# Turning q and k of two batches by 32x32 blocks on VectorE, with block copies in DRAM ahead of it

## The chip, the cores and the metric

The kernel runs on one core of a Trainium2 chip. The metric is the device time of one execution in microseconds (us); less is better. Where a profile is read, one execution was recorded by the hardware profiler, and its times count from the start of its span. TensorE does matrix products into PSUM, VectorE and ScalarE do elementwise work and read PSUM, GpSimd (POOL) does elementwise work on SBUF and issues indirect DMAs, and SyncE (SP) issues plain DMAs.

## The reference

Two parts, one after the other, in float32. First, linear attention with decay over q, k, v of shape (4 batches, 8 heads, 768 rows, 64):

```python
for b in range(nb):                      # blocks of 64 rows
    intra = np.einsum('bhic,bhjc->bhij', qb, kb) * Dmask
    intra = np.einsum('bhij,bhjd->bhid', intra, vb)
    inter = np.einsum('bhid,bhde->bhie', qb * lam_pow, kv_state)
    out[:, :, sl] = intra + inter
    kv_state = lam_block * kv_state + np.einsum('bhsd,bhse->bhde', kb_dec, vb)
```

The heads are then laid side by side: x has shape (4, 768, 512). Second, Fourier mixing and an MLP:

```python
mixed = np.real(np.fft.fft(np.fft.fft(x, axis=1), axis=2))
u = x + mixed
un = (u - mean(u)) / sqrt(var(u) + 1e-6)          # over the last axis
return u + np.maximum(un @ w_ch1, 0.0) @ w_ch2    # 512 -> 2048 -> 512
```

The weights come as float64; the kernel reads their bits and converts them on the chip.

## The kernel before, in words

**Attention.** `attn_chunk` (L257) handles 128 rows of one batch with all 8 heads; a batch has six chunks. It loads k, q and v of the chunk (L261, one DMA each, in runs of 256 B). The products of q and k need the head dimension on the partitions, so TensorE transposes k and q against an identity matrix, four 128x128 pieces each (L272, L277), and ScalarE copies the results to SBUF as kT and qT (L274, L279). VectorE makes qs, q with its decay, from the PSUM tile of q (L282). Then come the scores (L290), their decay on VectorE (sc, L294), the state update (L305, L309, L310), where kd, k with its decay, is made by GpSimd (L268), the two products into the output (L318 from qs and the state, L322 from sc and v), a copy oT (L325), and transposes back to row order (L329). ScalarE stores the result x to a scratch in DRAM, and indirect gathers on GpSimd fetch mirrored rows (`mirror_a` L377 and L380, `mirror_b` L385).

**Fourier part.** `fft_ln` folds rows with their mirror rows on VectorE (`fold_x`, L365 to L368, then L405 to L416), takes the transform over the rows as matrix products (L440), copies it out (L444), takes the transform over the width (`width`, L453 to L458, three row groups and one last row), adds it to x (L519 to L523), and normalises (`norm`: L470, L471, L474, L475, L487). For the first four pairs of batch and row group the result is transposed by TensorE (L492) for the MLP. For the other eight it is turned by blocks on VectorE (uq, L497) and written to DRAM (utd, L501), and the rows themselves go to DRAM as ud (L507).

**MLP, in two forms.** `mlp` (L549) does those first four pairs plainly: 64 products of the first weight (L555) with ReLU by ScalarE and VectorE in turn (L563, L561), and two lots of 16 products of the second (L569), each lot followed by the sum with x (L575, L576) and a store. Rows of the first half go out by a plain DMA on SP (L543), the mirrored rows by an indirect DMA on GpSimd (L545). `late` (L623) does the other eight pairs in four rounds with a scheme of seven products in place of eight on 2x2 blocks; it needs sums of the weights (`combine_weights`, L614) and of the inputs (us, L627 to L630), and its products are L637 and L684.

**What sets the order.** The program is written as generators that yield an estimated cost, and `weave` runs two of them side by side in a given ratio (L758 to L773). Weight conversion (L227 to L240) is woven into the first 190 us, the first form of the MLP into what is left of the attention and Fourier parts, `combine_weights` into the end of that MLP (L779). A scheduler in the build then orders the instructions of each engine by its own estimate of when their operands are there, and gives each engine a fixed list. Pools set how many tiles of a name exist: x has ten buffers in rotation (L127), y has one (L574), the loads of k, q and v have two.

Of the kernel before, what the change touches and what calls it, by code (L numbers as in the profile page):

```python
# [75 lines left out]
def kernel(  # L76
# [131 lines left out]
    w1v = moe_w_ch1.rearrange("(c p) f -> p c f", p=128)  # L208
    w2v = moe_w_ch2.rearrange("(c p) m -> p c m", p=128)
    WP = 512  # L210

    def load_tables(i):
        if i == 1:
# [5 lines left out]
    def load_weights(dst, src):  # L219

        if src.dtype == F32:
            nc.sync.dma_start(dst, src)
            return
        raw = hp_.tile([128, 2 * WP], U32, tag="hr", name=f"raw{cnt[0]}")
        pw = ep.tile([128, WP], U16, tag="pw", name=f"pw{cnt[0]}")
        cnt[0] += 1
        nc.sync.dma_start(raw, src.bitcast(U32))  # L227
        lo, hi = raw[:, 0:2 * WP:2], raw[:, 1:2 * WP:2]
        top = raw.bitcast(U16)[:, 3:4 * WP:4]
        lof, d = lo.bitcast(F32), dst.bitcast(U32)  # L230

        nc.vector.tensor_scalar(pw, top, 0x7FF0, None, op0=ALU.bitwise_and)
        nc.scalar.activation(pw, pw, AF.Relu, bias=cvt[:, 0:1], scale=-1.0)
        nc.scalar.activation(pw, pw, AF.Relu, bias=cvt[:, 1:2], scale=-8.0)
        nc.vector.scalar_tensor_tensor(pw, top, 0x8000, pw, op0=ALU.bitwise_and, op1=ALU.bitwise_or)  # L235

        nc.vector.tensor_scalar(d, hi, 0x000FFFFF, None, op0=ALU.bitwise_and)
        nc.scalar.activation(lof, lo, AF.Copy, scale=2.0 ** -52)
        nc.vector.scalar_tensor_tensor(dst, d, 2.0 ** -20, lof, op0=ALU.mult, op1=ALU.add)  # L239
        nc.vector.scalar_tensor_tensor(dst, dst, 1.0, pw.bitcast(BF16), op0=ALU.add, op1=ALU.mult)  # L240
# [8 lines left out]
            yield 1.0  # L249


    xs, xn_, xd = {}, {}, {}

    def pair(t, hp):
        return t[:, 2 * hp:2 * hp + 2, :].rearrange("p a d -> p (a d)")

    def attn_chunk(b, c):  # L257
        rows = slice(c * C, (c + 1) * C)
        kt, qt, vt = (new(ld, [C, H, D], nm) for nm in ("k", "q", "v"))
        for t, src in ((kt, k), (qt, q), (vt, v)):  # L260
            nc.sync.dma_start(t, src[b, :, rows, :].rearrange("h p d -> p h d"))  # L261
        if b == 0:
            load_tables(c)

        last = c == NC - 1
        if not last:
            kd = new(at, [C, H, D], "kd")
            nc.gpsimd.tensor_tensor(kd, kt, kpow, op=ALU.mult)  # L268

        ptk = psum_a([128, HP, C])  # L270
        for hp in range(HP):
            nc.tensor.transpose(ptk[:, hp, :], pair(kt, hp), ident)  # L272
        kT = new(at, [128, HP, C], "kT", bufs=2)
        nc.scalar.copy(kT, ptk)  # L274
        ptq = psum_a([128, HP, C])
        for hp in range(HP):
            nc.tensor.transpose(ptq[:, hp, :], pair(qt, hp), ident)  # L277
        qT = new(at, [128, HP, C], "qT", bufs=2)
        nc.scalar.copy(qT, ptq)  # L279
        if c > 0:  # L280
            qs = new(at, [128, HP, C], "qs")
            nc.vector.tensor_tensor(qs, ptq, qpow, op=ALU.mult)  # L282
        yield 1.2


        mm = nc.tensor.matmul
# [68 lines left out]
        nc.gpsimd.memset(t, 0.0)  # L355

    gather = nc.gpsimd.indirect_dma_start
    eo, r1s = {}, {}

    def fold_x(b, a, n, i, lo, hi):  # L360

# [8 lines left out]
    def mirror_a(b):  # L370

        xa = xd[b][0]
        r1 = r1s[b] = [new(fp, [128, DM], f"r{a}") for a in range(2)]

        eo[b] = [(new(fp, [128, 2, 2 * W], f"fe{a}"), new(fp, [128, 2, 2 * W], f"fo{a}")) for a in range(2)]
        for a, n in enumerate(BLK):
            gather(out=r1[a][0:n], out_offset=None, in_=xa[:, :], in_offset=row_of(a, n))  # L377
        for t in range(2, HC):
            u = xs[b, HC + t] = new(xp, [128, DM], "x")
            gather(out=u[:, :], out_offset=None, in_=xa[:, :], in_offset=row_of(2 + t))  # L380
# [6 lines left out]
            xs[b, t] = xn_.pop((b, t))  # L387

    def fold_a(b):
        r1 = r1s.pop(b)  # L390
        for a, n in enumerate(BLK):
            fold_x(b, a, n, 1, r1[a][0:n], xn_[b, HC + a][0:n])

    def fold_b(b):

# [145 lines left out]
    def store(b, T, y, cols=slice(0, DM)):  # L541
        if T < HC:
            nc.sync.dma_start(out[b, 128 * T:128 * T + 128, cols], y[:, cols])  # L543
        else:
            nc.gpsimd.indirect_dma_start(out=out.rearrange("b s d -> (b s) d"),  # L545
                                         out_offset=row_of(2 + HC * (b + 1) + T - HC),
                                         in_=y[:, :], in_offset=None)

    def mlp(b, g):  # L549
        ut = uts.pop((b, g))  # L550
        hr = []
        for fc in range(FO):
# [7 lines left out]
            if fc % 2:  # L560
                nc.vector.tensor_scalar(t, ps, 0.0, None, op0=ALU.max)  # L561
            else:
                nc.scalar.activation(t, ps, AF.Relu)  # L563
            yield 1.7
        for i in range(G):
            T = TT[g][i]
            ps = psum_m([128, DM])
            for fc in range(FO):
                nc.tensor.matmul(ps, lhsT=hr[fc // 4][:, fc % 4, 128 * i:128 * i + 128], rhs=w2[:, fc, :],  # L569
                                 start=(fc == 0), stop=(fc == FO - 1))  # L570
                if fc % 4 == 3 and fc < FO - 1:
                    yield 3.4
            u = xs.pop((b, T))
            y = new(up, [128, DM], "y", bufs=1)  # L574
            nc.vector.tensor_tensor(y[:, 0:HM], ps[:, 0:HM], u[:, 0:HM], op=ALU.add)  # L575
            nc.vector.tensor_tensor(y[:, HM:DM], ps[:, HM:DM], u[:, DM - 1:HM - 1:-1], op=ALU.add)  # L576
            store(b, T, y)
            yield 3.4


# [188 lines left out]

    run(weave(part(fr, 2 * t_chunk), weave(part(back, FO * 1.7 - 1.0), w, 0.9), 1.5))  # L770
    run(w)
    t_rest = 3 * t_front - 6 * t_chunk
    run(weave(fr, back, (len(PLAIN) * t_mlp - FO * 1.7 - 25.0) / t_rest))  # L773
    front_end.close()
    s2.wp = ctx.enter_context(tc.tile_pool(name="ws", bufs=1, side="left", reuse_waits="tile"))
# [43 lines left out]
```

## Time and profile before

| what | value |
|---|---|
| three runs | 878.85, 880.33, 881.35 us; median 880.33 |
| profiled execution, its own time | 881.11 us |
| its span | 879.1 us |
| mean granted TensorE clock | 0.981 |
| TensorE (matmul) busy | 805.4 us, 92% |
| VectorE busy | 444.6 us, 51% |
| ScalarE busy | 199.9 us, 23% |
| GpSimd busy | 89.0 us, 10% |
| moved by DMA | 72.43 MB in 129,407 packets |

How to read the lines that follow. A line of a group or of a timeline names the engine, the line of the kernel, the operation, and "out<-in" with the buffer numbers left out. PE is TensorE, PEld its weight loads, DVE VectorE, ACT ScalarE, and a "q" after an engine is its queue of DMA issues. In a timeline the first number is the start in us and the second the length. A bracket "[1.22 <-ACT ds L518]" says that the engine stood idle for 1.22 us and which instruction ended that. In a list of waits the numbers are us in total, times, longest. Matmuls overlap in the pipeline, so the time that one takes of a stream is the distance between the starts of its neighbours and not its own length. In a list of DMA queues the numbers are packets, MB and the share of the 16 DMA engines' time in the window.

In the span the weight conversion runs beside other work to about 189 us. Batch 0's attention comes first; batch 1's Fourier part ends, on TensorE, at 242.2; batch 2's attention runs from there to about 301, batch 3's from about 338 to 407. The last of the first-form MLP ends at 487.5, and the second form fills the rest.

### The profile page before, as it was taken

Reading aid. Unit: us, or ns where it says so; the run is one execution under the profiler, and the core shown is the slowest. Engines: PE = TensorE matmul, PEld = TensorE weight load, DVE = VectorE, ACT = ScalarE, POOL = GpSimd, SP = SyncE. Lnnn points to the kernel's source line nnn. Section 1 sums busy time; section 2 is a strip of 40 time slices with the busy share of each in tenths; the row PEclk is TensorE's granted clock in tenths of the full one; section 3 lists DMA queues with packets and bytes.
Section 4 is the critical chain, followed back from the end, with each engine's and each line's share of the span. In section 5 each row is a group of like instructions: output and inputs, shape, how many; then the busy total and the mean of one; then the engine's idle time right before and its main releaser. Section 6 shows DMA issues by size and latency. Waiting matters only on the chain.

```text
span 879.1 us, 11703 instructions
## 1 busy us (share of the span) xinstructions
PE 805.4 (92%) x4596; PEld 640.8 (73%) x4596; DVE 444.6 (51%) x1022; ACT 199.9 (23%) x451; POOL 89.0 (10%) x108
## 2 busy tenths in 40 slices
PE   4765768589999999999999999999999999999998
PEld 2654657454877657864884788888888888888886
DVE  4779869872562347434597354125611553135411
ACT  3665426630223102311210121002200220012100
POOL 2224311100021201102000000000000000000000
PEclk9998789899999999999999999999999999999999
DMA  9999325720065613643054101110111000110010
GB/s 229 244 239 262 82 81 143 235 72 24 25 137 130 161 37 109 123 94 102 37 141 110 25 1 48 48 48 1 44 40 45 16 1 1 48 48 1 1 37 24
DMA packets 129407, 72.43 MB, mean 82 GB/s; under 512 B 111264, under 2 KB 113832, under 8 KB 129352
## 3 DMA queue, kind: packets, MB, share of 16 engines
q1 hardware_dynamic: 123392, 57.51, 25.5%
q0 software_dynamic: 2496, 7.87, 2.8%
q10 hardware_dynamic: 3464, 6.30, 2.0%
q8 instruction: 36, 0.59, 0.3%
q14 instruction: 19, 0.16, 0.1%
HBM read 50.68 MB, written 20.99 MB: 82 GB/s over the span
## 4 chain that ended last, share of the span: by engine, by line
PE 70%; DVE 8%; issue 7%; DMA 4%; POOL 1%; ACT 0%; POOLq 0%; DVEq 0%; ACTq 0%
PE p L684 22%; PE p L637 22%; PE pm L555 8%; PE pm L569 7%; PE pa L440 3%; DMA raw<-in_moe_w_ch_dram 3%; PE pa L322 1%; PE pa L290 1%; DMA x<-xb,ix 1%; PE pa L318 1%; PE pa L305 1%; DVE pw L235 1%; DVE w L239 1%; DVE w L240 1%; PE pa L329 1%
## 5 line engine op out<-in xcount | busy, mean ns | idle before, releaser
L555 PE MATMUL pm<-ut,w 128*128 128x256 f32 x512 | 123.4, 390 | 10.7 <-ACT hr L563 9.0
L555 PEld LDWEIGHTS pm<-ut,w 128*128 128x128 f32 x512 | 95.1, 193 | 28.2 <-ACT hr L563 10.1
L569 PE MATMUL pm<-w,hr 128*128 128x512 f32 x256 | 114.8, 596 | 0.0
L637 PE MATMUL p<-ur,w 128*128 128x256 f32 x384 | 93.6, 379 | 0.1
L569 PEld LDWEIGHTS pm<-w,hr 128*128 128x128 f32 x256 | 47.0, 190 | 51.8 <-issue 51.2
L637 PEld LDWEIGHTS p<-ur,w 128*128 128x128 f32 x384 | 72.9, 190 | 10.7 <-issue 0.5
L637 PE MATMUL p<-us,w1s 128*128 128x256 f32 x256 | 65.2, 379 | 0.0
L684 PE MATMUL p<-w,hs 128*128 128x256 f32 x256 | 58.0, 379 | 0.5 <-DVE y L705 0.5
L684 PE MATMUL p<-w,ha 128*128 128x256 f32 x256 | 57.9, 379 | 0.0
L684 PE MATMUL p<-w2s,hs 128*128 128x256 f32 x256 | 57.9, 379 | 0.0
L684 PEld LDWEIGHTS p<-w,hs 128*128 128x128 f32 x256 | 48.5, 190 | 7.5 <-DVE y L705 0.9
L684 PEld LDWEIGHTS p<-w2s,hs 128*128 128x128 f32 x256 | 48.6, 190 | 6.6
L684 PEld LDWEIGHTS p<-w,ha 128*128 128x128 f32 x256 | 48.6, 190 | 6.6
L637 PEld LDWEIGHTS p<-us,w1s 128*128 128x128 f32 x256 | 48.6, 190 | 6.6
L545 POOL DMA_INDIRECT out_dram<-y,ix x12 | 11.8, 982 | 404.9 <-DVE y L710 344.2
L664 ACT COPY ha<-p 128x256 f32<-128x256 f32 x32 | 11.9, 372 | 172.8 <-PE p L637 172.8
L322 PE MATMUL pa<-sc,v 128*64 128x128 f32 x384 | 32.1, 291 | 10.7 <-DVE sc L294 10.7
L282 DVE TENSOR_TENSOR qs<-pa,qpow 128x512 f32<-128x512 f32 x20 | 13.8, 689 | 51.2 <-ACT qT L279 51.2
L290 PE MATMUL pa<-qT,kT 64*128 64x128 f32 x384 | 29.4, 291 | 10.1 <-ACT qT L279 10.1
L290 PEld LDWEIGHTS pa<-qT,kT 64*128 64x128 f32 x384 | 24.5, 193 | 19.1 <-ACT qT L279 15.8
L322 PEld LDWEIGHTS pa<-sc,v 128*64 128x64 f32 x384 | 23.8, 143 | 18.8 <-DVE sc L294 13.8
L675 DVE TENSOR_TENSOR ha<-p,ha 128x256 f32<-128x256 f32 x32 | 13.6, 425 | 45.6 <-ACT ha L674 45.4
(142 smaller groups left out, 1188.5 us busy)
## 6 DMA issues: line engine op xcount, KB each, us to landing
raw<-in_moe_w_ch_dram SPq DMA_DIRECT2D x32, 512.0 KB, 5.9
k<-in_k_dram SPq DMA_DIRECT2D x24, 256.0 KB, 5.1
q<-in_q_dram SPq DMA_DIRECT2D x24, 256.0 KB, 4.0
v<-in_v_dram SPq DMA_DIRECT2D x24, 256.0 KB, 4.2
ud<-x SPq DMA_DIRECT2D x16, 256.0 KB, 2.2
utd<-uq SPq DMA_DIRECT2D x64, 64.0 KB, 2.2
u<-ud SPq DMA_DIRECT2D x16, 256.0 KB, 2.6
ur<-utd SPq DMA_DIRECT2D x8, 512.0 KB
```

The source lines that it names most:

```text
L235: nc.vector.scalar_tensor_tensor(pw, top, 0x8000, pw, op0=ALU.bitwise_and, op1=ALU.bitwise_or)
L282: nc.vector.tensor_tensor(qs, ptq, qpow, op=ALU.mult)
L290: mm(pss[hi][:, hp, :], lhsT=kT[HD[hi], hp, :], rhs=qT[HD[hi], hp, :], start=True, stop=True)
L322: mm(po[HD[hi], hp, :], lhsT=vt[:, 2 * hp + hi, :], rhs=sc[hi][:, hp, :], start=(c == 0 and hp == 0), stop=(hp == HP - 1), skip_group_chec ...
L440: mm = nc.tensor.matmul(ps[0:m, n, :], lhsT=piece(a, i, n), rhs=cs[0:rows, a, i in (2, 3), n, :], start=(a == 0), stop=(a == 1))
L545: nc.gpsimd.indirect_dma_start(out=out.rearrange("b s d -> (b s) d"), out_offset=row_of(2 + HC * (b + 1) + T - HC), in_=y[:, :], in_offset ...
L555: nc.tensor.matmul(ps, lhsT=w1[:, c, 128 * fc:128 * fc + 128], rhs=ut[:, c, :], start=(c == 0), stop=(c == KO - 1))
L569: nc.tensor.matmul(ps, lhsT=hr[fc // 4][:, fc % 4, 128 * i:128 * i + 128], rhs=w2[:, fc, :], start=(fc == 0), stop=(fc == FO - 1))
L637: nc.tensor.matmul(ps, lhsT=s2.A[a][:, kt, 128 * i:128 * i + 128], rhs=U[b][:, kt, :], start=(first and kt == 0), stop=(kt == 1), skip_gro ...
L664: nc.scalar.copy(a11, two(X))
L675: V.tensor_tensor(a22, two(Z), a22, op=ADD)
L684: nc.tensor.matmul(ps, lhsT=h[a][:, s, i, :], rhs=s2.B[b][:, i, :], start=(first and i == 0), stop=(i == HF - 1), skip_group_check=True)
```

## The change

For batches 2 and 3 (`TURNED`), q and k are no longer transposed by TensorE. Three things take its place.

`move_blocks` copies q and k of a batch from DRAM to DRAM in runs of 32 numbers (128 B), so that the 32x32 blocks which make up the transpose lie in the right order: 32 DMAs of 768 runs each for a batch. Batch 2's 32 are issued together, and wait for the last weight piece's first conversion step (L232 before). Batch 3's are issued in four lots of eight, one with each of batch 2's chunks 0 to 3, and each lot waits for that chunk's last turn.

A chunk then loads its blocks of k and q (128 partitions, runs of 2 KB) and turns them with one `nc.vector.transpose` each; the results are kT and qT. The natural k is still loaded for kd except in the last chunk, the natural q is not. qs is made from qT.

Stores of mirrored rows in the first form of the MLP are held, and issued when the next group has done its fifth step; y has two buffers instead of one. The gathers of `mirror_a` write into a part of the fold's tile instead of a tile of their own. The ratio by which the MLP is woven in is worked out anew for the smaller estimate of a chunk.

```diff
+    def move_blocks(b, hps, after):
+        for nm, src in (("k", k), ("q", q)):
+            if (b, nm) not in moved:
+                moved[b, nm] = dram.tile([4, 32, NC, 4, HP, 32], F32, name=f"moved_{nm}{b}")
+            for a in range(4):
+                for hp in hps:
+                    i = nc.sync.dma_start(moved[b, nm][a, :, :, :, hp].rearrange("n c t d -> n (c t) d"),
+                                          src[b, 2 * hp + a // 2, :, 32 * (a % 2):32 * (a % 2) + 32]
+                                          .rearrange("(t n) d -> n t d", n=32))
+                    tc.add_manual_dep(i.ins, after.name, mybir.DependencyInfo(
+                        mybir.DependencyClass.Sync, mybir.DependencyReason.DATA))
...
+        def turned(nm, load, src, bufs):
+            t = new(ld, [128, HP * C], load, bufs=bufs)
+            nc.sync.dma_start(t, moved[b, src][:, :, c].rearrange("a n t h d -> a n (t h d)"))
+            tT = new(at, [128, HP, C], nm, bufs=2)
+            turns.append(nc.vector.transpose(tT.rearrange("p h (t n) -> p h t n", t=4),
+                                             t.rearrange("p (t h d) -> p h t d", h=HP, t=4)).ins)
+            return tT
+        if blocks:
+            kT, qT = turned("kT", "kb", "k", 1), turned("qT", "q", "q", 2)
+            ptq = qT
+            if not last:
+                kt = natural("k", k)
...
+        if b in TURNED and b + 1 in TURNED and c < 4:
+            move_blocks(b + 1, (c,), turns[-1])
...
-        yield 1.2
+        yield 0.3 if blocks else 1.2
...
-            gather(out=r1[a][0:n], out_offset=None, in_=xa[:, :], in_offset=row_of(a, n))
+            gather(out=eo[b][a][1][0:n, 1, 0:DM], out_offset=None, in_=xa[:, :], in_offset=row_of(a, n))
...
+            if fc == 4:
+                while held:
+                    store(*held.pop())
...
-            y = new(up, [128, DM], "y", bufs=1)
+            y = new(up, [128, DM], "y", bufs=2)
...
-            store(b, T, y)
+            if T < HC or (b, g) == PLAIN[-1]:
+                store(b, T, y)
+            else:
+                held.append((b, T, y))
...
     run(w)
-    t_rest = 3 * t_front - 6 * t_chunk
+    move_blocks(TURNED[0], range(HP), conv[-1])
+    t_rest = 3 * t_front - 6 * t_chunk - 0.9 * NC * len(TURNED)
     run(weave(fr, back, (len(PLAIN) * t_mlp - FO * 1.7 - 25.0) / t_rest))
```

## The prediction

> **What bounds the kernel now.** I read the page's shares first, then the busy time by stage, then TensorE and VectorE in order of time at the seam before the last stage, then waits and DMA. Page and stages (the columns of the second are span, then busy us of PE, PEld, DVE, ACT, POOL, then clock, DMA share, GB/s):
>
> ```profile
> PE 805.4 (92%) x4596; PEld 640.8 (73%) x4596; DVE 444.6 (51%) x1022; ACT 199.9 (23%) x451; POOL 89.0 (10%) x108
> ```
> ```profile
> 186.00:242.20 56.20, 53.79 (x212) 34.07 (x210) 24.34 (x59) 7.92 (x23) 3.85 (x5) 1.00 0.06 19
> 242.20:407.00 164.80, 160.07 (x1219) 114.56 (x1219) 78.23 (x175) 37.18 (x90) 28.39 (x36) 1.00 0.48 114
> 407.00:451.00 44.00, 43.15 (x195) 31.69 (x194) 27.02 (x69) 6.98 (x23) 5.10 (x9) 1.00 0.25 71
> 451.00:487.50 36.50, 36.50 (x108) 20.11 (x107) 27.05 (x35) 1.15 (x3) 0.60 (x1) 1.00 0.46 117
> 487.50:879.10 391.60, 387.40 (x1793) 340.06 (x1791) 142.59 (x390) 48.00 (x128) 8.75 (x9) 1.00 0.08 26
> ```
> From 242 us TensorE is the bound: of 636.9 us it is idle 9.8, of which 5.6 before 487.5. So what TensorE is spared there shortens the end, if other work still fills its waits. What fills them at the seam is the first form of the MLP:
>
> ```profile
> 397.91 0.60 PE L272 MATMUL pa<-ident,k 128*128 128x128 f32 x4
> 398.35 0.60 PE L277 MATMUL pa<-ident,q 128*128 128x128 f32 x4
> 398.78 1.02 PE L569 MATMUL pm<-w,hr 128*128 128x512 f32 x2
> ...
> 444.35 15.81 PE L555 MATMUL pm<-ut,w 128*128 128x256 f32 x72
> 460.00 27.63 PE L569 MATMUL pm<-w,hr 128*128 128x512 f32 x64
> 487.46 6.52 PE L637 MATMUL p<-ur,w 128*128 128x256 f32 x28
> ```
> ```profile
> 433.38 0.42 DVE L519 TENSOR_TENSOR ds<-pa,bs 128x256 f32<-128x256 f32 x1 [1.22 <-ACT ds L518]
> ...
> 451.64 2.36 DVE L614 TENSOR_TENSOR w1s<-w 128x1024 f32<-128x1024 f32 x2 [1.13 <-POOL rs L475]
> ...
> 472.95 0.69 DVE L629 TENSOR_TENSOR us<-ur,us 128x512 f32<-128x512 f32 x1
> ```
> The reader is to see that batch 3's attention ends at 407 (its last L329), and that from its Fourier fold to the weight sums of L614 there is a chain of some 65 us, mostly VectorE's, ahead of the last stage's products. All of it lies under L555 and L569.
>
> **What the Trainium skill says.** *DMA: Bandwidth & Descriptors*, Specifications, gives 512 B as the least run for full rate. The trace agrees that short runs are slow (prices below). The same page, Anatomy of one DMA, says that a wait is held by the issuing sequencer before dispatch: so what stands behind a waiting copy on SP waits too, as SP's 52.4 us at L261 for L322 show. *VectorE: DVE Perf Modes*, The three transpose paths, says that VectorE turns 32x32 blocks only; hence the block copies. L497 is such a turn here, 702 ns for 128x512. Neither page prices a copy from DRAM to DRAM.
>
> **The change, part by part.** An engine here runs a fixed list, in the order of the built program; in the profile each fp32 matmul of that list except transposes counts twice. I compared the two lists.
>
> *Turns off TensorE.* Eight transposes in each of 12 chunks go. Four of L272 start 0.44 us before L277, so one takes 0.109 us of the stream: 96 x 0.109 = 10.5 us less, all where TensorE is the bound. ScalarE loses 24 copies of 0.59 (14 us), none on the path. VectorE gains 24 turns of 0.70, 17 us in the stretch where it is busy 78 of 165 us, and qs then reads SBUF instead of PSUM; hidden beside TensorE's work: 0 taken, 17 at most if each turn were waited for.
>
> *Block copies.* Batch 2's are 32 DMAs of 768 runs of 128 B behind the last L232 (about 185.5 us); batch 3's are 8 behind the turns of each of chunks 0 to 3. The nearest rows:
>
> ```profile
> q1 hardware_dynamic: 1508, 0.20, 36.9%
> ```
> ```profile
> q1 hardware_dynamic: 1040, 0.26, 19.2%
> ```
> The first is 261 to 264.5 us, almost only utd writes in runs of 128 B: 0.369 x 16 x 3.5 us / 1508 = 13.7 ns of engine time a run. The second is 269 to 275, one k load in runs of 256 B: 17.7 ns. A copy reads and writes DRAM: 14 ns if both overlap, 31 if they add; I take 20. Batch 2: 24,576 x 20 ns / 16 = 31 us (21 to 48), and 32 issues of some 0.65 us (L501's pace on SP), so done by 207 to 234. In the new lists the first load of blocks stands on SP behind a VectorE turn that follows the first output of the second MLP group, near 275 us: hidden. Passed on SP are the output store of 201.4 (its buffer is doubled) and utd and ud writes, which have no reader before 450. But the two gathers of batch 1's mirror (202 and 219 us, 3.4 us each) now share the DMA engines: +2 (0 to 6). Batch 3's copies are 6,144 runs, 8 us at 20 ns (5 to 12), per chunk, with the next chunk's loads behind them on SP; the new list puts 28 us of MLP between chunks 0 and 1 (59 L597 at 0.432, 3 L614 at 0.859), 15 between 1 and 2, and 17 ahead of chunk 4; chunk 3's loads stand ahead of chunk 2's copies: hidden. Both batches' copies come on the path above some 60 ns a run: for batch 2, 98 us from 185.5 until its first turn is due, over 1,536 runs on each DMA engine. No gain is possible from a copy that was not there.
>
> *Stores one group later.* The long POOL waits are not the stores' doing:
>
> ```profile
> POOL x L385 <- DVE y L576: 75.5, 4, 39.3
> ```
> The gather waits for a buffer of x that L576 still reads, not for a store ahead of it. The 37.1 us wait of L545 at 488.7 has nothing behind it. Value 0, gain at most the 1 us that one issue takes ahead of a wanted step. Gathering into fo instead of r: 0.
>
> *What the order moves.* This decides. In the new lists batch 2's chunks wait for copies, and the MLP is drawn forward into the gap. After batch 1's Fourier part TensorE has 34 L597, 32 L614 (the new numbers of L555, L569), then chunk 0, then 59 L597 ahead of chunk 1. When batch 3's last chunk ends, no L597 or L614 is left (before: 25 us of them between 407 and 444, then 43 us in one piece). Costs, from 242.2 us on:
> - Work: 245.3 - 5.6 = 239.7 busy; less 10.5, less about 4.5 for some 45 fewer changes between kinds of matmul (four L555 take 0.96 after a change, 0.87 in a run): 224.7. Of this the last Fourier part is 11.1 (L440 40 x 0.175, widths 4.1), so 213.6 ahead of it.
> - The ReLU of the second L597 step stands on VectorE behind all of batch 1's norms, which end at 251 in the trace (last L470 from 249.73, 1.26 for two); with three banks of PSUM TensorE stops after ten L597, at 242.2 + 10 x 0.432 = 246.5: +5 (0 to 6).
> - Within chunks with little MLP between them, TensorE waits for sc and oT (0.68 and 0.59 a piece): about 0.3 in each of batch 2's, 6 in batch 3's with VectorE's norms in front of its first sc; batch 2's Fourier part has only 10 us of L614 for its fold: +2. Sum +10 (4 to 18).
> - So batch 3's attention ends at 242.2 + 2 + 213.6 + 5 + 10 = 473.
> - Tail: fold begins 6.9 us after the last L329 (407.1 to 414.0), the first ds 14.7 us later when nothing but the fold and L440 is in the way (9.2 fold, 3.6 L440 left, 1.9 widths and copies): 21.6. From the first ds to the last us is 433.38 to 473.6 = 40.2; less eight ReLUs at 0.33 and a 0.5 wait that leave, plus two pieces of L614 (1.14 each) that now come ahead: 39.4. The first product that needs weight sum and us (built as seventh to start) begins at 473 + 61 = 534. Of these 61 us TensorE works 11 and 2: +48 (36 to 58).
> - The rest is the last stage: 391.6 less the 1.7 done = 389.9. Span 534 + 390 = 924.
>
> The profiled execution was 881.1 for a span of 879.1, 0.8 above the median of 880.3: 924 + 2.0 - 0.8 = 925. Sum against before: -10.5 - 4.5 + 2 + 5 + (10 - 5.6) + 48 = +44. I say 924.
>
> **Rivals.** *Copies too slow.* If a run costs 80 ns, 20 over the 60 that are hidden, batch 2 loses 1,536 x 20 ns = 31 us and batch 3 as much: 924 + 61 = 985. For it: DRAM on both sides, not seen here. Against it: 13.7 and 17.7.
> *Faster: the saving without the tail.* TensorE keeps its 10.5 and 4.5, and the fold, norms and weight sums of batch 3 stay under MLP work as they do now: 880 - 15 + 5 for the rest = 870. For it: 99% busy now, and VectorE has room. It wins if over 35 us of MLP is still unissued when batch 3's attention ends. Against it: the list has none there.
> *A small tail.* The list is as read but the chunks run so much sooner that the tail costs below 15 us: 890 or less, as low as no change. Against it: its length is a chain of VectorE work with durations from this trace.
>
> **Chances.** Forecast 0.86 (own range 903 to 950: tail -12 or +10, chunks -6 or +8, ReLU -5 or +1, gathers -2 or +4, clock of TensorE after the idle stretch up to 5, not all at once); slow copies 0.07; faster 0.04; small tail 0.03, two thirds of it within 0.3%. 0.3% is about what a measurement of this kernel tells from no change. Faster 0.05, same 0.02, slower 0.93. Range 902 to 952: it leaves out the slow copies and the faster case.
>
> **What would show it.** Right: no L597 or L614 after batch 3's last L371; TensorE idle some 45 us in one stretch there, VectorE busy in it with L559 to L563 and L663; the last stage unchanged at about 390 us; batch 2's first kb load landed before its turn is due. Wrong, if DVE waits for kb or q loads (copies over 60 ns a run), if the stretch is short, or if POOL's stores now hold kd.

## The result, and the profile after

The changed kernel takes 939.66 us in the median of four runs (934.81 to 941.28), against 880.75 us of the kernel before (also four runs). The ratio is 1.0664, with a 95% interval of 1.062 to 1.0707: slower by some 59 us. The forecast was 924 with a range of 902 to 952. The profiled execution took 934.81 us for a span of 933.0, and is the fastest of the four; the median lies 4.9 us above it.

The page's line of shares comes first. TensorE is busy for as long as before (808.8 against 805.4 us), although 96 transposes are gone, and it stands idle for 124 us of the span instead of 74:

```profile
PE 808.8 (87%) x4500; PEld 640.7 (69%) x4500; DVE 462.2 (50%) x1046; ACT 186.6 (20%) x427; POOL 86.8 (9%) x108
```

By stage, with the columns as before (span; busy us of PE, PEld, DVE, ACT, POOL; granted clock; DMA share; GB/s):

```profile
182.30:240.30 58.00, 54.60 (x216) 34.80 (x214) 25.32 (x61) 8.62 (x24) 2.84 (x4) 1.00 0.38 68
240.30:394.00 153.70, 152.81 (x832) 106.24 (x832) 44.89 (x94) 15.75 (x40) 12.65 (x16) 1.00 0.38 90
394.00:424.00 30.00, 25.52 (x104) 15.84 (x102) 17.64 (x40) 4.68 (x15) 5.21 (x5) 0.89 0.39 117
424.00:472.10 48.10, 43.37 (x413) 28.58 (x412) 35.90 (x74) 7.35 (x19) 11.51 (x15) 0.96 0.61 155
472.10:497.80 25.70, 13.51 (x76) 10.86 (x76) 15.75 (x37) 4.68 (x15) 4.87 (x5) 0.73 0.27 75
497.80:534.60 36.80, 3.79 (x9) 2.52 (x8) 34.74 (x57) 0.60 (x3) 3.30 (x6) 0.61 0.45 125
534.60:933.00 398.40, 390.22 (x1784) 341.85 (x1784) 143.85 (x392) 47.79 (x128) 7.80 (x8) 0.99 0.10 29
```

Batch 2's attention now lasts to 394 with TensorE full (152.8 of 153.7 us), where it ended at 302 before. Batch 3's ends at 472.1 instead of 407. From there to 534.6 TensorE works 17.3 of 62.5 us, while VectorE is busy for 34.7 of the last 36.8. TensorE in order of time over that stretch shows no L597 or L614, the lines that covered it before:

```profile
484.29 1.63 PE L480 MATMUL pa<-cs,fe 128*128 128x193 f32 x4 [12.21 <-DVE fe L449]
...
497.46 0.38 PE L496 MATMUL pa<-dt,ys 128*1 128x128 f32 x2
512.16 3.75 PE L686 MATMUL p<-ur,w 128*128 128x256 f32 x8 [14.32 <-DVE uq L537]
534.65 8.22 PE L686 MATMUL p<-ur,w 128*128 128x256 f32 x24 [18.74 <-DVE ur L679]
547.25 4.89 PE L686 MATMUL p<-us,w1s 128*128 128x256 f32 x14 [4.38 <-ACT ha L713]
```

The brackets are the new waits: 12.2 us for the fold, 14.3 and 18.7 us for norms and weight sums, then 4.4 us for a copy of ScalarE. VectorE's chain in the same time answers to the one shown before, with the first ds, a weight sum and the last piece of us and ur:

```profile
495.43 0.43 DVE L559 TENSOR_TENSOR ds<-pa,bs 128x256 f32<-128x256 f32 x1 [5.13 <-ACT ds L558]
...
516.01 2.35 DVE L663 TENSOR_TENSOR w1s<-w,w1s 128x1024 f32<-128x1024 f32 x2
...
533.92 0.68 DVE L679 TENSOR_TENSOR ur<-ur 128x512 f32<-128x512 f32 x1
```

From first ds to last ur it lasts 39.2 us, as the forecast had it (39.4), but almost nothing on TensorE lies beside it. SP's queue shows how copies, writes and block loads follow each other ahead of batch 2 (start, length and line of its DMA issues):

```profile
182.81 12.06 SPq L265 DMA_DIRECT2D moved_k<-in_k_dram  x16
194.91 12.00 SPq L265 DMA_DIRECT2D moved_q<-in_q_dram  x16
207.01 0.58 SPq L583 DMA_DIRECT2D out_dram<-y  x1
245.97 2.65 SPq L541 DMA_DIRECT2D utd<-uq  x4
248.66 2.09 SPq L547 DMA_DIRECT2D ud<-x  x4
271.86 2.59 SPq L541 DMA_DIRECT2D utd<-uq  x4
274.49 0.62 SPq L288 DMA_DIRECT2D kb<-moved_k  x1
```

All 32 copies of batch 2 are issued by 207 us, at 0.75 us each, and each lands 3.1 us after its issue in the median. Yet the first block load (kb) goes out at 274.49, behind the utd writes. In 182.8 to 207 the DMA queue carried

```profile
q1 hardware_dynamic: 23391, 2.94, 75.8%
```

that is 0.758 x 16 x 24.2 us / 23,391 = 12.5 ns of engine time a run, less than the forecast's 20.

Late loads are not what the engines wait for here, though. The second chunk of batch 2 shows it, with its load on SP, its turn on VectorE and its scores on TensorE:

```profile
295.21 0.64 SPq L288 DMA_DIRECT2D kb<-moved_k  x1
...
315.93 0.42 DVE L603 TENSOR_SCALAR hr<-pm 128x256 f32<-128x256 f32 x1 [2.96 <-PE pm L597]
316.27 0.70 DVE L290 STREAM_TRANSPOSE kT<-kb 128x512 f32<-128x512 f32 x1
...
318.40 1.16 PE L332 MATMUL pa<-qT,kT 64*128 64x128 f32 x16
```

A kb load lands 3.1 us after its issue in the median, so this one was there some 18 us before its turn. The turn stands in VectorE's list behind the ReLUs of the MLP (L603), which wait for TensorE, and TensorE is full. In the whole run VectorE waits 3.4 us for kb and 1.8 us for q. So in this execution the built order holds batch 2's chunks back; what the copies have to do with that order, the experiments show.

### The profile page after: what moved, and what is told of

Its sections match the earlier page's. It is cut to its first block, busy times and chain, and to the rows that moved or that the text cites. A ratio compares the mean times of both kernels' runs of the same rounds, so it can differ in the third digit from the quotient of the medians.

```text
span 933.0 us, 11574 instructions
## 1 busy us (share of the span) xinstructions
PE 808.8 (87%) x4500; PEld 640.7 (69%) x4500; DVE 462.2 (50%) x1046; ACT 186.6 (20%) x427; POOL 86.8 (9%) x108
## 4 chain that ended last, share of the span: by engine, by line
PE 70%; DVE 14%; DMA 7%; issue 2%; ACT 2%; SPq 1%; POOL 1%; DVEq 0%; POOLq 0%; ACTq 0%
PE p L733 21%; PE p L686 20%; PE pm L614 9%; PE pm L597 8%; PE pa L480 4%; DMA raw<-in_moe_w_ch_dram 3%; PE pa L364 2%; DMA x<-xb,ix 2%; PE pa L332 1%; DVE pw L236 1%; PE pa L360 1%; PE pa L371 1%; SPq L541 1%; DMA utd<-uq 1%; DVE w L240 1%
## 5 line engine op out<-in xcount | busy, mean ns | idle before, releaser
L597 PE MATMUL pm<-ut,w 128*128 128x256 f32 x512 | 119.7, 388 | 9.6 <-ACT hr L605 7.2
L686 PE MATMUL p<-ur,w 128*128 128x256 f32 x384 | 98.2, 394 | 33.1 <-DVE ur L679 18.7
L614 PE MATMUL pm<-w,hr 128*128 128x512 f32 x256 | 116.0, 603 | 0.0
L597 PEld LDWEIGHTS pm<-ut,w 128*128 128x128 f32 x512 | 96.5, 193 | 27.5 <-ACT hr L605 8.4
L686 PEld LDWEIGHTS p<-ur,w 128*128 128x128 f32 x384 | 75.9, 198 | 45.0 <-DVE ur L679 19.5
L614 PEld LDWEIGHTS pm<-w,hr 128*128 128x128 f32 x256 | 47.7, 192 | 53.5 <-issue 53.0
L686 PEld LDWEIGHTS p<-us,w1s 128*128 128x128 f32 x256 | 49.6, 194 | 11.9 <-ACT ha L713 4.8
L585 POOL DMA_INDIRECT out_dram<-y,ix x12 | 12.2, 1019 | 426.0 <-DVE y L759 378.1
L603 DVE TENSOR_SCALAR hr<-pm 128x256 f32<-128x256 f32 x32 | 13.3, 418 | 61.2 <-PE pm L597 61.1
L336 DVE TENSOR_TENSOR sc<-pa,decay 128x512 f32<-128x512 f32 x48 | 31.2, 680 | 17.8 <-PE pa L332 14.8
L480 PE MATMUL pa<-cs,fe 128*128 128x193 f32 (+3 forms) x96 | 21.9, 374 | 19.4 <-DVE fe L449 19.1
```

The costliest lines, as they stand in the source:

```text
L336: nc.vector.tensor_tensor(t, pss[hi], decay[:, hi::2, :], op=ALU.mult)
L480: mm = nc.tensor.matmul(ps[0:m, n, :], lhsT=piece(a, i, n), rhs=cs[0:rows, a, i in (2, 3), n, :], start=(a == 0), stop=(a == 1))
L597: nc.tensor.matmul(ps, lhsT=w1[:, c, 128 * fc:128 * fc + 128], rhs=ut[:, c, :], start=(c == 0), stop=(c == KO - 1))
L686: nc.tensor.matmul(ps, lhsT=s2.A[a][:, kt, 128 * i:128 * i + 128], rhs=U[b][:, kt, :], start=(first and kt == 0), stop=(kt == 1), skip_gro ...
```

## The experiments

Theory 1 is the prediction's: the built order brings the MLP forward, and the tail behind batch 3's attention is left bare. Its rivals are that copies, block reads or turns cost the time themselves. The first four kernels were to tell these apart.

**hold_a.** The changed kernel with its last MLP group kept behind batch 3:

```diff
-                nc.tensor.matmul(ps, lhsT=w1[...], rhs=ut[:, c, :], ...)
+                m = nc.tensor.matmul(ps, lhsT=w1[...], rhs=ut[:, c, :], ...)
+                if (b, g) == PLAIN[-1] and c == 0:
+                    tc.keep_in_program_order(m)
```

The same mark is put on every fourth product of w2 in that group and on the first score product of each chunk of batch 3.

> The changed kernel with one edit: the MLP group of batch 1 that is the last of PLAIN is kept on TensorE behind batch 3's attention, so that its first products lie between the Fourier matmuls of batch 3 and its 36 + 32 last matmuls behind them, as in the kernel before. Copies, turns on VectorE and held stores stay. Theory (the order left nothing to cover the tail, worth about 48 us and its slow clock): 880 to 900 us, above 880 by what batch 3's chunks now wait for, since they lose their few MLP matmuls (6 chunks of 1 to 3 us), the wait before the first product of the last stage under 5 us. Rival (copies, blocks read back in 128-byte runs or the turns themselves cost the time): 930 to 945 us, the tail's idle time only moved to another place.

Measured: 934.08 us, ratio 1.0597 (1.0562 to 1.0632). The tail is covered: no wait of L692, the first products of the last stage, is left. But the idle time came up elsewhere (us in total over the span, times, longest):

```profile
PE pa L482 <- DVE fe L451: 31.6, 3, 16.6
PE pa L366 <- DVE sc L338: 17.7, 10, 6.5
PE pa L373 <- ACT oT L369: 12.0, 17, 1.0
```

Of these, 29.4, 9.0 and 6.1 us lie behind 240 us: at the folds of batches 2 and 3, and at chunks that have now no MLP beside them, batch 3's above all. Batch 2's first chunks still have the MLP of other groups between them, and the last of them ends its attention at 381. Taking 55 us of MLP out from ahead of batch 3 (64 x 0.432 + 32 x 0.859, the forecast's own pace) brought the end of its attention forward by 12.5 us only (471.4 to 458.9). Theory 1 falls as a cause by itself: the bare tail is what is seen, but to cover it brings 6 us of 59.

**hold_e.** As hold_a, with the last two groups, (0,0) and (1,1), marked in the same way (`if (b, g) in PLAIN[2:]`).

> The changed kernel with the last two MLP groups of PLAIN, (0,0) and (1,1), held in the order of the program against batch 3's chunks, its Fourier matmuls and its width products, so that they lie among batch 3's attention and behind it much as in the kernel before. Batch 2's chunks and its Fourier stage are left without MLP. Theory (the place of the MLP sets the time): the tail is covered and batch 3's chunks too; batch 2's are bare instead: 880 to 905 us, with 10 to 25 us idle at batch 2's chunks and Fourier stage. Rival (copies, reads or turns cost it): 930 us or more.

Measured: 930.94 us, 1.0559 (1.0524 to 1.0594), so again the rival's number. Tail and batch 3 are covered as before, and batch 2 is bare: its fold waits 15.5 us, and its scores wait 9.8 us for kT and 8.6 for qT. Here the block loads do come late. SP issues the second chunk's kb at 302.09, behind utd writes and copies, and VectorE, which has stood idle for 10.4 us, turns it at 305.70. In 240 to 400 us TensorE is idle for 49.6 us, about the whole loss.

**copies_only.** The kernel before, with the copies and nothing that reads them (batch 3's lots are tied to the copy to qT, cp, as there are no turns):

```diff
+        if b in TURNED and b + 1 in TURNED and c < 4:
+            move_blocks(b + 1, (c,), cp.ins)
...
+    move_blocks(TURNED[0], range(HP), conv[-1])
```

> The kernel before with one part of the change: the 64 block copies are issued at the same places and tied in the same way, but nothing reads them; q and k are turned on TensorE as before, no turns on VectorE, stores at once. The built order on TensorE is again one with no MLP matmul among or behind batch 3's chunks, since the loads stand behind the copies on SP's queue. Theory (the copies' place on the queue alone makes the builder draw the MLP forward): 925 to 960 us, about as slow as the changed kernel or slower, idle at batch 2's and batch 3's Fourier folds and ahead of the last stage. Rival (the turns on VectorE, the reads of the blocks or the wait for them cost it): 878 to 890 us, since the copies' transfers themselves have room.

Measured: 978.55 us, 1.1097 (1.106 to 1.1135), slower than the changed kernel by 39 us and beyond the expected 960. Copies alone, unread, with all transposes still on TensorE and no turns on VectorE, make more than the whole loss. Here batch 1's Fourier part is stretched as well (its second part of L461 starts at 274.7 us, against 224.7 for L440 before), which the changed kernel avoids. In its trace the last gather of that batch's fold waits 46.7 us, until 249.5, for a buffer of x that a sum of the MLP frees; why the order puts it there was not tried.

**stores_only.** The kernel before with held stores, two y buffers, and gathers into fo:

```diff
-            gather(out=r1[a][0:n], out_offset=None, in_=xa[:, :], in_offset=row_of(a, n))
+            gather(out=eo[b][a][1][0:n, 1, 0:DM], out_offset=None, in_=xa[:, :], in_offset=row_of(a, n))
...
-            store(b, T, y)
+            if T < HC or (b, g) == PLAIN[-1]:
+                store(b, T, y)
+            else:
+                held.append((b, T, y))
```

> The kernel before with one part of the change: the indirect stores are issued one group later with two y buffers, and the early gathers land in the fold's own buffer. The order on TensorE is the kernel before's. Theory (held stores free nobody, as loads of x still wait for their buffers): 877 to 884 us, no difference that can be measured. Rival (holding them back costs, by buffers kept longer or by a later gather): 888 us or more.

Measured: 883.75 us against 882.94, 1.0005 (0.9986 to 1.0023). This part of the change is worth nothing, as forecast.

Theory 2 then was that the front end (attention, Fourier stage and norms of batches 2 and 3) is what ends last, and that it is late by the wait for batch 2's first blocks. Four kernels followed.

**wait4.** The kernel before with a wait alone (uqs lists the turned blocks of the norms, L497):

```diff
+            if (b, c) == (2, 0):
+                tc.add_manual_dep(i.ins, uqs[-1].name, mybir.DependencyInfo(
+                    mybir.DependencyClass.Sync, mybir.DependencyReason.DATA))
```

> The kernel before with a wait alone: the loads of k, q and v of batch 2's first chunk wait for the last turned normalised block (uq) of batch 1; no copies, no turns of q and k on VectorE, stores at once. Theory formed after the first four runs (the front end, that is attention, Fourier stage and norms of batches 2 and 3, is what ends last; the MLP is a fixed store of cover for it; what is lost is the delay of batch 2's first chunk, about 40 us): batch 2's first attention matmul moves from 245 us to 275 to 290, the MLP is run solid ahead of it, and the total is 905 to 930 us. Rival 1 (the place of the MLP in the order alone, the tail being covered by 22 + 32 matmuls here): 880 to 890 us. Rival 2 (turns or block reads cost it): 880 us.

Measured: 890.09 us, 1.0133 (1.0097 to 1.0168): a miss, 15 us below the range. Batch 2's first scores came at 281.2, 36 us late, as was meant. But then its chunks followed each other every 8.2 us in the mean (9.3 before, both by their last transposes), since the MLP done in the meantime was no longer due between them, and batch 3's attention ended only 14.6 us late (421.2 against 406.6). So the MLP can absorb most of a late start, if nothing slows the chunks that come after.

**plain_reads.** The changed kernel without copies, its turned loads reading 2 KB runs from q and k:

```diff
-            nc.sync.dma_start(t, moved[b, src][:, :, c].rearrange("a n t h d -> a n (t h d)"))
+            src = {"k": k, "q": q}[src].rearrange("b h s d -> b (h s d)")
+            nc.sync.dma_start(t, src[b, c * 65536:(c + 1) * 65536].rearrange("(p e) -> p e", p=128))
```

> The changed kernel without the block copies: each turned load reads a contiguous piece of q or k of the same size in runs of 2 KB (so the attention of batches 2 and 3 is computed on misplaced data), and nothing is copied. Turns on VectorE, held stores and gathers stay. Theory (delay of batch 2's first chunk through the copies): the first chunk starts by 245 us, the order has the MLP among and behind batch 3's chunks again, 862 to 875 us, below the kernel before by the TensorE transposes saved. Rival (turns on VectorE cost it, as they lengthen each chunk's chain and queue before the folds): 890 us or more.

Measured: 883.27 us against 879.70, 1.004 (1.0022 to 1.0058). Without copies the loss is gone, with turns, held stores, gathers and the new ratio all in place: 3.6 of 59 us are left. But the saving isn't there either. Batch 2's last chunk ends 3.1 us sooner than before (298.4), and its Fourier part starts 4.2 us later. GpSimd's timeline shows what is in between:

```profile
301.36 0.99 POOL L420 DMA_INDIRECT x<-xa,ix  x1 [0.30 <-issue]
310.58 0.95 POOL L425 DMA_INDIRECT x<-xb,ix  x1 [8.23 <-DVE y L620]
```

The last gather of the fold needs a buffer of x that the sum with y of the MLP still reads, and that sum waits for MLP products on TensorE. In the kernel before, the same gather goes out at 306.21. So what the transposes left free did not reach the front end, which waited for the MLP here. That more buffers of x would turn this into a gain was not tried.

**after_act.** The changed kernel with one word changed:

```diff
-                    i = nc.sync.dma_start(moved[b, nm][a, :, :, :, hp].rearrange("n c t d -> n (c t) d"),
+                    i = nc.scalar.dma_start(moved[b, nm][a, :, :, :, hp].rearrange("n c t d -> n (c t) d"),
```

> The changed kernel with one word changed: the block copies are issued from ScalarE's queue in place of SyncE's. Copies, their ties, the reads of blocks, turns and held stores stay. The built order on TensorE then has batch 2's first chunk right behind batch 1's last width products, and 36 + 32 MLP matmuls behind batch 3's Fourier stage, as in the kernel before. Theory (delay of batch 2's front end by loads that stand behind the copies and other entries on SP's queue): batch 2's first attention matmul by 255 us, 865 to 890 us, the upper end if 32 issues of 0.75 us hold up ScalarE's ReLUs near 185 to 210 us. Rival (the copies' transfers or the turns cost the time): 925 us or more, as nothing of either is taken away.

Measured: 911.76 us, 1.0365 (1.0334 to 1.0395), between the two. Batch 2's first scores came at 264.7, not by 255. ScalarE's queue says why:

```profile
190.30 17.52 ACTq L265 DMA_DIRECT2D moved_k<-in_k_dram  x14
207.86 27.15 ACTq L265 DMA_DIRECT2D moved_q<-in_q_dram  x16
235.06 0.29 ACT L441 COPY fe<-fe 128x2 f32<-128x2 f32 x2 [44.04 <-DMA moved_q<-in_q_dram]
```

For 45 us the engine issues copies, and its first step for batch 1's fold stands behind them; L480 of batch 1 starts at 236.8 instead of 206.9. Copies, reads and turns are all there, and 28 us are won back by another queue and the order that comes with it: the transfers themselves are not what costs these.

**direct16_he.** No copies, 16 loads of 128-byte runs for each tensor and chunk, and the last two MLP groups marked as in hold_e:

```diff
-            nc.sync.dma_start(t, moved[b, src][:, :, c].rearrange("a n t h d -> a n (t h d)"))
+            for a in range(4):
+                for e in range(HP):
+                    nc.sync.dma_start(
+                        t[32 * a:32 * a + 32].rearrange("p (t h d) -> p t h d", h=HP, t=4)[:, :, e, :],
+                        natural_src[b, 2 * e + a // 2, c * C:(c + 1) * C, 32 * (a % 2):32 * (a % 2) + 32]
+                        .rearrange("(t n) d -> n t d", n=32))
```

> The changed kernel without the copies: each turned load is made of 16 DMAs that read q or k directly in runs of 128 bytes, and the last two MLP groups of PLAIN are held in the order of the program against batch 3's chunks. Theory: batch 2's first chunk starts by 250 us and the tail is covered: 865 to 885 us, where above 875 then because 32 issues a chunk keep SP busy. Rival (reads in 128-byte runs and turns cost it): 900 us or more.

Measured: 959.32 us, 1.0888 (1.0826 to 1.095): a miss, through issues again. Batch 2 started by 249.8 as expected, but then SP's queue set the pace:

```profile
417.93 9.56 SPq L291 DMA_DIRECT2D kb<-in_k_dram  x16
427.53 7.59 SPq L291 DMA_DIRECT2D q<-in_q_dram  x16
436.32 8.02 SPq L291 DMA_DIRECT2D kb<-in_k_dram  x16
444.38 9.11 SPq L291 DMA_DIRECT2D q<-in_q_dram  x16
```

A DMA of 128 runs takes about 0.5 us to issue, against 0.75 for one of 768. So a chunk's 32 loads take 17 us of SP, and batch 3's scores come 18 to 29 us apart. TensorE waited 49.6 us for qT.

Theory 3 was formed from these eight: the MLP is a store of cover that absorbs the late start, but not the second delay, batch 3's copies among batch 2's loads. Its three kernels split the change by batch and by queue.

**turn2** (batch 2 alone is turned) and **turn3** (batch 3 alone, with each lot of its copies tied to a chunk's copy to qT instead of a turn):

```diff
-    TURNED = range(2, B)
+    TURNED = range(2, 3)
```
```diff
-    TURNED = range(2, B)
+    TURNED = range(3, B)
...
-    move_blocks(TURNED[0], range(HP), conv[-1])
```

> The changed kernel with batch 2 alone turned on VectorE: its 32 copies behind the weights stay, batch 3's copies are gone and batch 3 is turned on TensorE as before. Theory after eight runs (the MLP is a store of cover; batch 2's front end is late by 35 to 40 us through the wait for its first blocks, which the store can still absorb, and by some 50 more through batch 3's 32 copies among batch 2's loads, which it can't): batch 2's first attention matmul at 275 to 290 us, its chunks then every 7 to 10 us, the MLP left for the end (30 + 32 matmuls): 885 to 900 us. Rival (the first wait, or turned chunks as such, make the loss): 915 us or more.

> The changed kernel with batch 3 alone turned on VectorE: batch 2 is turned on TensorE as before and has no copies ahead of it; batch 3's 32 copies stand among batch 2's loads, each group of 8 tied to a chunk of batch 2. Theory (batch 3's copies among batch 2's loads stretch batch 2): its first attention matmul by 250 us, but its last chunk at 370 us or later, against 302 in the kernel before, and no MLP left for the end but 5 matmuls: 910 to 935 us. Rival (the first wait makes the loss): 880 to 890 us.

Measured: turn2 889.37 us, 1.0089 (1.0063 to 1.0116); turn3 923.69 us, 1.0465 (1.0406 to 1.0524). Both are in the theory's range. In turn2 the first scores come at 289.5 and the last transposes of batch 2 at 328.5. In turn3 the first come at 247.7, 3 us later than before, and the last at 376.8; the copies make 23 us of issues on SP, and the loads stand between them:

```profile
284.45 0.58 SPq L282 DMA_DIRECT2D q<-in_q_dram  x1
...
286.01 1.22 SPq L282 DMA_DIRECT2D k<-in_k_dram  x1
318.22 2.62 SPq L265 DMA_DIRECT2D moved_k<-in_k_dram  x4
320.88 3.02 SPq L265 DMA_DIRECT2D moved_q<-in_q_dram  x4
324.00 0.58 SPq L282 DMA_DIRECT2D q<-in_q_dram  x1
324.68 1.65 SPq L282 DMA_DIRECT2D v<-in_v_dram  x1
```

Each lot waits for the chunk that it is tied to, and the next loads wait behind the lot: SP issues nothing from 287.2 to 318.2, and the copies go out as the third chunk's scores begin (318.4). But 23 us of issues don't make batch 2 end 75 us later than before (301.5). TensorE works 139.2 of the 140 us from 240 to 380; between the third chunk's transposes of k and of q its list has 50 us of MLP:

```profile
266.62 0.60 PE L312 MATMUL pa<-ident,k 128*128 128x128 f32 x4
...
271.81 27.63 PE L614 MATMUL pm<-w,hr 128*128 128x512 f32 x64
299.27 17.86 PE L597 MATMUL pm<-ut,w 128*128 128x256 f32 x82
316.97 0.60 PE L317 MATMUL pa<-ident,q 128*128 128x128 f32 x4
```

That q was issued at 284.45, over 30 us before its transposes. So here, too, the copies act through the built order: with them among the loads, the list draws the MLP ahead of chunks. That it does so because the scheduler expects these loads late fits the way it orders work, but no run shows its estimates.

**split.** All copies kept, batch 3's on another queue:

```diff
-                    i = nc.sync.dma_start(moved[b, nm][a, :, :, :, hp].rearrange("n c t d -> n (c t) d"),
+                    i = (nc.sync if b == 2 else nc.scalar).dma_start(
+                        moved[b, nm][a, :, :, :, hp].rearrange("n c t d -> n (c t) d"),
```

> The changed kernel with batch 3's 32 copies alone issued from ScalarE's queue; batch 2's stay on SyncE's. All copies, ties, block reads, turns and held stores stay. Theory: batch 2 starts late as in the changed kernel (275 to 290 us) but its chunks follow every 7 to 12 us, since its loads no longer stand behind copies, and the MLP is left for the end: 885 to 905 us, the upper end if ScalarE's 32 issues of 0.75 us hold up its copies from PSUM. Rival (transfers of the copies, block reads or turns cost the time): 925 to 945 us.

Measured: 901.7 us, 1.0191 (1.0114 to 1.0268). Of 59 us 38 are won back with every copy, read and turn in place. Part of the rest is ScalarE held by issues: oT waits there behind them, and TensorE waits for oT (us in total, times, longest; 15.6 of it in three waits in batch 2), where the changed kernel has 7.5 us in 10 waits:

```profile
PE pa L371 <- ACT oT L367: 21.7, 11, 6.9
```

**warm_tail.** The changed kernel with 34 products that nobody reads in the idle stretch ahead of the last stage, for a term that the forecast had in its range but not in its sum (next section):

```diff
+    idle = psum_a([128, 2 * NK])
+    for _ in range(34):
+        nc.tensor.matmul(idle, lhsT=ident, rhs=ys[3][:, 0:2 * NK], start=True, stop=True)
     front_end.close()
```

> The changed kernel with 34 matmuls more whose result nobody reads (identity with batch 3's first-stage columns, 386 wide), placed on TensorE between the last width product of batch 3 and the first product of the last stage, where it sits idle for 33 us. Theory (the lower granted clock after the idle stretch adds some 3 us to the first 24 products after it): the first 24 products take 5.2 to 6.0 us in place of 8.2, the granted clock there is over 0.9, the total is 2 to 5 us below the changed kernel: 934 to 938 us. Rival (the products are slow there for another reason, such as their weights or their order): they take 8 us again, total 939 to 941 us, or more if the added matmuls end too late (535 us and after).

Measured: 942.08 us, 1.0719 (1.0657 to 1.078). Inconclusive. The added products ended at 525.5, but VectorE's weight sums waited 5.2 us for the last of them, and with the chain that follows 21.75 us of idle time stood ahead of the 24 products all the same; they took 7.13 us instead of 8.22. It doesn't show what a warm start would bring.

**All runs by three marks.** From the timeline of TensorE of each run: batch 2's first scores, the start of its last transposes of oT, that of batch 3's last transposes of oT, and the span left after that.

| run | span | batch 2 first | batch 2 last | batch 3 last | rest |
|---|---|---|---|---|---|
| before | 879.1 | 245.0 | 301.5 | 406.6 | 472.5 |
| plain_reads | 879.1 | 245.4 | 298.4 | 406.3 | 472.8 |
| stores_only | 880.5 | 246.4 | 302.9 | 408.0 | 472.4 |
| wait4 | 883.3 | 281.2 | 327.4 | 421.2 | 462.1 |
| turn2 | 886.5 | 289.5 | 328.5 | 422.3 | 464.2 |
| split | 900.8 | 293.3 | 352.6 | 434.9 | 465.9 |
| after_act | 912.0 | 264.7 | 325.8 | 439.5 | 472.5 |
| turn3 | 922.4 | 247.7 | 376.8 | 458.4 | 464.0 |
| hold_e | 929.5 | 291.6 | 350.6 | 455.8 | 473.7 |
| hold_a | 932.0 | 290.1 | 380.5 | 458.9 | 473.1 |
| after | 933.0 | 284.5 | 393.5 | 471.4 | 461.6 |
| warm_tail | 940.2 | 290.1 | 399.0 | 477.0 | 463.2 |
| direct16_he | 958.5 | 249.8 | 335.8 | 484.7 | 473.8 |
| copies_only | 978.9 | 295.0 | 427.4 | 518.2 | 460.6 |

The rest is 461 to 474 us in all fourteen. It is near 473 where a whole MLP group lies behind batch 3's attention, and 461 to 466 where none or only part of one does. So the end of batch 3's attention sets the time, and a tail with a whole group of MLP behind it is only some 11 us longer than a bare one. What moves that end is the pace of batch 2 and batch 3, not its first start: wait4 and turn2 start 36 to 44 us late and lose 15 to 16 us at batch 3's end, turn3 starts 3 us late and loses 52.

## Why the prediction was right, and where it was not

Sign and range were right, and so was the course of events: the MLP is drawn forward, batch 3's attention ends late and the tail is bare. Some of the sum came out by luck, and the forecast took for the cause what is one half of it.

- **Copies.** A run cost 12.5 ns, not 20. As transfers and as waits the copies are hidden, as forecast: in 240.3 to 394 us TensorE is idle 0.9 us. What failed is to price batch 3's copies, with the loads behind them on SP, at nothing: turn3 has those copies alone and loses 4.65%, and split moves them off SP and wins back 38 us. The forecast said that chunks wait for copies and that the MLP fills the gap, and it counted the MLP between batch 2's chunks (28, 15 and 17 us), but as work moved, not as the delay of the front end that it stands for.
- **Turns off TensorE, 10.5 + 4.5 us.** "All where TensorE is the bound" failed: plain_reads has the saving and no copies, and is 0.4% slower. In 182 to 407 us its TensorE is busy 210.0 us against 215.6 before, and the stretch is no shorter; the fold's gather waits for an x buffer that the MLP frees. The forecast knew that wait from GpSimd's list and used it for the stores only. In the changed kernel the work itself shrank by less: TensorE is busy 235.3 us from 240.3 until the last stage's products, with the same MLP products as in the 239.7 us before, so 4.4 us less and not 15. The lower granted clock takes part of that: the 80 records of L480 in that time take 18.6 us, those of L440 before 14.9.
- **Stores.** 0 forecast, 1.0005 measured. GpSimd's wait for x is still there (before 75.5 us in 4 waits):

```profile
POOL x L426 <- DVE y L621: 53.5, 2, 36.6
```

- **Gathers, +2.** Not seen: batch 1's Fourier part ends at 240.3, before at 242.2. Both are within what the weight stage varies by: L440 or its like starts between 203 and 217 us in all runs but after_act.
- **ReLU behind the norms, +5.** Mis-sized: the stops near 247 and 249.5 us sum to 0.9. **Chunks and Fourier part, +10:** idle in 394 to 472.1 is 4.5 + 4.7 = 9.2. Batch 3's attention ended at 472.1 for 473, but by luck: TensorE worked 221.7 us up to there, 8.1 more than the forecast's 213.6, and this was made up by a start 3.9 us earlier (240.3 for 242.2 + 2) and by stops that are 4.9 us shorter (10.1 for 15).
- **Tail, +48.** The product that was to need the weight sums and the last piece of the inputs (in the trace it waits for ur) starts at 534.65 for 534, and from 472.1 to 534.6 TensorE is idle 45.2 us, in three stops and not in one stretch. Size and place were right. As a cause by itself it was wrong: the forecast's faster case "wins if over 35 us of MLP is still unissued when batch 3's attention ends", and hold_a leaves 55 us unissued there and takes 934 us. The MLP moved forward and the late front end go together; put back, it leaves the late front end bare.
- **Last stage, 390.** The mis-sized term of the sum: 398.4. The first 24 products take 8.22 us, 0.343 each, where this line goes at 0.216 later, so 3.0 us; the next 14 take 4.89, where 14 at 0.249 would be 3.48 as in warm_tail, so 1.4; and 4.4 us TensorE waits between them for ScalarE's first copy, which follows the last utd write of the norms (issued by 545). Before, L569 covered that write. The forecast had the clock after the idle stretch, up to 5 us, in its range only.
- **From span to median.** 1.8 us lie around the span, and the profiled execution was 4.9 us below the median: 6.7 where the forecast took 1.2. Together: 924 + 8.4 + 0.6 of the first product + 1.8 around the span + 4.9 = 939.7.

So the loss comes from the copies by way of their place on the queue that issues them, and with SP's queue it shows in one of two forms. In the changed kernel the built order holds batch 2's chunks, and the loads are nearly all there before their turns. With the MLP out of the way, in hold_e, the chunks wait for block loads behind copies, and TensorE is idle 18.4 us for kT and qT. What stays open is whether a better order exists with these copies on SP: no run had them there with the order of the kernel before. No version here beats the kernel before; the bound that plain_reads gives, without any copies, is no gain.

## What to carry to other kernels

Work that fills an engine's waits is a store: ask first which chain ends last, and price a change by how far it moves the end of that chain, since in hold_a and hold_e filler put back where it was missed only bared another place. Count the DMA issues of a change against the queue that its next loads share, and look for them between the loads, not only ahead of the first; a DMA of 16 KB in 128 runs took about 0.5 us of that queue here, one of 96 KB in 768 runs 0.75. When a queue looks like the cause, see on the engine itself whether a late load is what it waits for: in the changed kernel it was not. Before a resource is credited with a saving, follow what the next chain waits for: here a gather waited for a buffer that the filler itself had to free.

## What the runs showed of the hardware

- **Issue cost.** An SP issue took 0.75 us for 768 runs of 128 B and about 0.5 us for 128 runs. On ScalarE the same copies took 1.25 to 1.7 us each in 190 to 235 us (17.52/14 and 27.15/16), and while they were issued no other ScalarE instruction ran.
- **Copies in DRAM.** A copy from DRAM to DRAM in runs of 128 B took 12.5 ns of DMA engine time a run, against the 13.7 ns of utd writes from SBUF (one window each).
- **TensorE's clock.** In the changed kernel the granted clock in short windows from 534.6 us is

```profile
534.60:537.00 2.40, 2.35 (x6) 1.90 (x7) 0.40 (x1) 0.00 (x0) 0.00 (x0) 0.50 0.39 63
537.00:539.00 2.00, 2.00 (x6) 1.63 (x5) 1.05 (x3) 0.00 (x0) 0.00 (x0) 0.50 0.18 28
539.00:541.00 2.00, 2.00 (x8) 1.60 (x7) 0.00 (x0) 0.00 (x0) 0.00 (x0) 0.68 0.64 98
541.00:543.00 2.00, 1.87 (x9) 1.31 (x7) 0.71 (x1) 0.00 (x0) 0.00 (x0) 1.00 0.04 6
```

that is half until some 540.3 us, 5.6 us after the restart. After the shorter wait at 547.25 it is half again until about 550.5, 3.3 us. The Trainium skill's page *TensorE: Matmul & The Clock Gate*, in the section What's actually happening, gives half rate after an idle window and about 3.4 us of sustained work to leave it, in windows of fixed length that don't start with the work. The second restart agrees with 3.4 us; the first took longer, which fits the rest of one window and a whole one. A wait of 4.4 us was enough here to lose the full clock.
